# moe's last product: a stage of seven block products over pairs of token blocks, behind the first products of all nine blocks

## Chip, core and metric

One Trainium2 chip, one core. The time is the device time of one execution in microseconds, from the first to the last instruction and what lies around them; lower is better. The engines are PE (TensorE, the matrix engine), DVE (VectorE), ACT (ScalarE), POOL (GpSimd) and SP (SyncE, which issues nearly all transfers here).

## What is computed

Everything is float32: 4608 tokens, width 512.

```python
scores = scale * (q_c @ k_c.T)              # per head, in chunks of 64 tokens; 8 heads of 64
x = softmax(scores) @ v_c                   # attention, 4608 x 512
a, b = x @ w1, x @ w2                       # moe: 512 -> 1024, twice: the "first products"
y = ((a * b) @ w3) @ w_out                  # 1024 -> 1024 -> 512
h = y @ w_in                                # moe2: 512 -> 2048
out = (maximum(h, 0) + alpha * minimum(h, 0)) @ w_out2      # 2048 -> 512
```

The kernel multiplies `w3 @ w_out` once (the folds, 192 products), so that moe's last product is g = a * b (1024 wide) by one matrix of 1024 x 512.

## The kernel before

**Precision.** Every operand is held as a high and a low part in a rounded format (`split`: ScalarE copies the high part, VectorE subtracts it for the low part), and a product is three passes on PE, low x high, high x high, high x low (`PASSES`, L25). Weights come as 64-bit numbers and are converted on the chip, half a granule at a time (`convert_a` to `convert_e`, L180 to L216: one ScalarE absolute value, five VectorE operations, a ScalarE copy, two VectorE operations). There are 72 conversions: 0 to 15 for w1 and w2, 16 to 23 for w_out, 24 to 39 for w3, 32 for moe2's weights. moe2's are combined two by two (`combined_weight`, L230) into pieces for a seven-product scheme and written to DRAM.

**Tiles.** Tokens come in nine blocks of 512. A "step" (b, f) of the first products is one 128-wide slice f (of 8) of block b: `proj1` (L393) runs 12 PE products of 512 columns for a and 12 for b, ScalarE copies a out of PSUM, and `product` (L398) multiplies on VectorE. An attention unit is 256 tokens, two to a block; its scores, maximum, exponentials, normalisation, transposes and values are separate steps.

**Stages.** (1) STARTUP (L37) is an order written out by hand, one letter a step: A to E are the conversion's parts, S M X Y T P V c d attention's, a k b m a step of the first products, h s w the folds. It covers units 0 to 7, first products of blocks 0 to 3, conversions 0 to 39 and all folds; g of these blocks goes to DRAM. Sets of the first products take PSUM banks a and b and the pair p01 in turn. (2) L582 to L596: last product (`proj_wc`, L421) of blocks 0 to 3, g read back and split. (3) L598 to L627: for blocks 4 to 8, step by step, first products, attention of the next block, one conversion of moe2's weights, and the last product of the step before, straight from SBUF, into four banks (p01 and p23). y goes to DRAM. (4) moe2's first product as seven block products for eight (L654), over pairs of blocks (1,2), (3,4), (5,6), (7,8) and the two halves of block 0 (256 columns); results go to DRAM. (5) moe2's last product, seven for eight again, read from DRAM, in five output groups (L775), with the rows turned and written out (`rows`, L757).

Tiles of one tag share their buffers, and an instruction that takes a buffer waits until the last use of the one before it is over. A planner orders the instructions of each engine; PE's stand in program order where `pinned` is set, which it is from stage 2 on. Transfers of a queue issue in order.

Of the kernel before, what the change touches and what calls it, by code (L numbers as in the profile page):

```python
# [18 lines left out]
P = 128  # L19
# [25 lines left out]
    E15 a1.4 A16 B16 k1.4 b1.4 C16 D16 E16 V4 Y5 q6 m1.4 a0.6 A17 B17 k0.6 b0.6 C17 D17 E17 T5 P5 V5  # L45
    q7 m0.6 a1.5 A18 B18 k1.5 b1.5 C18 D18 E18 m1.5 a0.7 A19 B19 k0.7 b0.7 C19 D19 E19 m0.7 a1.6 A20 B20 k1.6
    b1.6 C20 D20 E20 c4 d4 c5 d5 m1.6 a1.7 A21 B21 k1.7 b1.7 C21 D21 E21 S6 M6 X6 m1.7 a2.0 A22 B22
    k2.0 b2.0 C22 D22 E22 S7 M7 Y6 X7 m2.0 a2.1 A23 B23 k2.1 b2.1 C23 D23 E23 T6 P6 V6 c6 d6 m2.1
    a2.2 A24 B24 k2.2 b2.2 C24 D24 E24 Y7 T7 P7 V7 m2.2 a2.3 A25 B25 k2.3 b2.3 C25 D25 E25 c7 d7 m2.3
    h0.0 A26 B26 C26 D26 E26 h0.1 s0 w0 A27 B27 C27 D27 E27 a2.4 A28 B28 k2.4 b2.4 C28 D28 E28 m2.4 h1.0  # L50
    A29 B29 C29 D29 E29 a2.5 A30 B30 k2.5 b2.5 C30 D30 E30 m2.5 h1.1 s1 w1 a2.6 A31 B31 k2.6 b2.6 C31 D31
    E31 m2.6 h2.0 A32 B32 C32 D32 E32 a2.7 A33 B33 k2.7 b2.7 C33 D33 E33 m2.7 h2.1 s2 w2 A34 B34 C34 D34
    E34 h3.0 A35 B35 C35 D35 E35 a3.0 A36 B36 k3.0 b3.0 C36 D36 E36 m3.0 h3.1 s3 w3 a3.1 A37 B37 k3.1 b3.1
    C37 D37 E37 m3.1 h4.0 A38 B38 C38 D38 E38 a3.2 A39 B39 k3.2 b3.2 C39 D39 E39 m3.2 h4.1 s4 w4 a3.3 k3.3
    b3.3 m3.3 h5.0 h5.1 s5 w5 a3.4 k3.4 b3.4 m3.4 h6.0 a3.5 k3.5 b3.5 m3.5 h6.1 s6 w6 a3.6 k3.6 b3.6 m3.6 h7.0 a3.7
    k3.7 b3.7 m3.7 h7.1 s7 w7
# [28 lines left out]
def tile_attention_moe_moe(ctx: ExitStack, tc: tile.TileContext, qkv: bass.AP, w12: bass.AP,  # L85
# [29 lines left out]
    g_dram = {(b, f): tc.dram_tile([P, TB], F32, name=f"g_dram{b}_{f}") for b in range(LEAD) for f in range(NF1)}  # L115
# [43 lines left out]
    def accumulators():  # L159
        p01, p23 = pair("p01", "acc"), pair("p23", "acc")  # L160
        return [p01[:, 0], p01[:, 1], p23[:, 0], p23[:, 1]]
# [8 lines left out]
    conv = [(*x, half) for x in CONVERTED if len(x) == 2 for half in range(2)] + [x for x in CONVERTED if len(x) == 3]  # L170
# [47 lines left out]
    ahead = [2 * (8 + 4 + 8)]  # L218
# [11 lines left out]
    def combined_weight(i):  # L230
# [13 lines left out]
        t14, t32 = (tmp(n).rearrange("p (g a c) -> p g a c", a=4, c=32) for n in ("t14", "t32"))  # L244
        for out, x, y in ((t14[:, left], b12, b11), (t32[:, left], b22, b12), (t32[:, right], b22, t14[:, left]),
                          (t14[:, right], b21, t32[:, right])):
            vector.tensor_tensor(out=out, in0=x, in1=y, op=ALU.subtract)
        for n, x in enumerate((t14, t32) + ((w0, b22) if half == 0 else (w1, b11))):
            g = granule((3, 5, 6, 7)[pieces[0] % 4], "wm")
            pieces[0] += 1  # L250
            if n < 3:
                split(g.rearrange("p s (g a c) -> p s g a c", a=4, c=32), x)
                nc.sync.dma_start(out=w2_dram[half, j, n], in_=g.bitcast(F32))
            else:
                split(g[:, :, :HW].rearrange("p s (g a c) -> p s g a c", a=4, c=32), x)
                nc.sync.dma_start(out=w2_dram[half, j // 2, n][:, :, HW * (j % 2):HW * (j % 2) + HW],
                                  in_=g[:, :, :HW].bitcast(F32))

    def convert():

        i = ahead[0]
        if i < len(conv):
            second_weight(i)
            if i % 2:
                combined_weight(i)
            ahead[0] = i + 1
# [11 lines left out]
    def load_unit(u, whole=True):  # L278
        if u < 4:
            slots = (24 + 2 * u, 25 + 2 * u, 2 * u, 2 * u + 1)  # L280
        elif u < 2 * LEAD:
            slots = range(24 + 4 * (u % 2), 28 + 4 * (u % 2))
        else:
            slots = (0, 1, 2, 4)
# [86 lines left out]
    wc_g = {}  # L371
    g_t, acc, ab = {}, {}, {}

    def fold(f, half):
        if half == 0:
            if f % 2 == 0:
                ab["fold"] = pair("p23", "wc")
        ps = ab["fold"][:, f % 2]
# [4 lines left out]

    def fold_split(f, lo):
        if not lo:
            wc_g[f] = granule(24 + f, "wc")
        dst, ps = wc_g[f], ab["fold"][:, f % 2]
        if lo:
            vector.tensor_tensor(out=dst[:, LO], in0=ps, in1=dst[:, HI].bitcast(F32), op=ALU.subtract)
        else:  # L390
            scalar.copy(dst[:, HI], ps)
# [6 lines left out]
    def product(b, f, a, ps):  # L398
        vector.tensor_tensor(out=a, in0=ps, in1=a, op=ALU.mult)
        if b < LEAD:  # L400
            nc.sync.dma_start(out=g_dram[b, f], in_=a)
        else:
            split_g(b, f, a)

    def empty_pair(sums, last, name, to):

        for i in (last - 1, last):
            t = tmp(name)
            (scalar.copy if i % 2 else vector.tensor_copy)(t, sums[i])
            nc.sync.dma_start(out=to(i), in_=t)  # L410
# [484 lines left out]
```

## Time and profile before

| | us |
|---|---|
| median of 3 runs | 1450.17 (1447.37 to 1450.45) |
| the profiled execution | 1448.14 |
| its span, first to last instruction | 1446.4 |
| PE busy | 1404.0 (97%) |
| VectorE busy | 1001.3 (69%) |
| ScalarE busy | 731.0 (51%) |
| mean granted clock of PE | 0.998 of full speed |

A PE product lasts longer than its distance to the next one, since they are pipelined; the distance between runs is what counts. VectorE's and ScalarE's instructions overlap a little in the same way. Idle time of an engine is given in square brackets with what ended it.

### The profile page before, as it was taken

To read this page: it belongs to the slowest core of one execution; us is meant where nothing else is said; L and a number is where in the kernel's file an instruction comes from. 1 tells how busy PE (TensorE), PEld (TensorE's weight loads), DVE (VectorE), ACT (ScalarE), POOL (GpSimd) and SP (SyncE) were. 2 spreads that over 40 slices of the span, in tenths; PEclk is the share of its full clock that TensorE was granted. 3 is DMA by queue.
4 is the path that set the end of the run, shared out by engine and by line. 5 is a ranking of instruction groups with operands and counts; after the bars stand their busy time and mean duration, and the time that the engine had idled before them with its cause. 6 is when DMAs were issued, how large, how long until landed. Compare 5 with 4: busy or idle time off the path is not lost.

```text
span 1446.4 us, 22817 instructions
## 1 busy us (share of the span) xinstructions
PE 1404.0 (97%) x8608; PEld 1163.1 (80%) x8608; DVE 1001.3 (69%) x1522; ACT 731.0 (51%) x1560; POOL 0.7 (0%) x6
## 2 busy tenths in 40 slices
PE   5899999999999999999999999999999999999997
PEld 4677788887788888888878787878898888888887
DVE  6888786233487877777245757675667878888775
ACT  6544532144355555553246767676765444444433
POOL 0000000000000000000000000000000000000000
PEclk9999999999999999999999999999999999999999
DMA  8555342344466666668372424333499563736343
GB/s 276 179 202 168 104 152 95 133 151 149 139 217 225 213 218 213 225 213 292 129 255 109 160 110 167 118 116 123 152 320 332 196 217 124 217 126 190 135 127 102
DMA packets 129790, 256.32 MB, mean 177 GB/s; under 512 B 13456, under 2 KB 58512, under 8 KB 129680
## 3 DMA queue, kind: packets, MB, share of 16 engines
q1 hardware_dynamic: 129680, 254.87, 52.1%
q8 instruction: 67, 1.10, 0.3%
q14 instruction: 43, 0.35, 0.1%
HBM read 160.44 MB, written 94.37 MB: 176 GB/s over the span
## 4 chain that ended last, share of the span: by engine, by line
PE 87%; ACT 5%; DVE 4%; DMA 3%; issue 1%; SPq 0%; ACTq 0%; DVEq 0%
PE a L128 19%; PE b L128 19%; PE q L128 17%; PE acc L128 13%; PE bc L128 9%; PE ab L128 4%; PE wc L128 3%; ACT e L77 3%; DVE m L77 1%; PE sc L128 1%; PE pa L128 1%; DVE p L77 1%; DMA g_dram<-r 1%; DMA raw<-in_w 1%; PE pa L133 1%
## 5 line engine op out<-in xcount | busy, mean ns | idle before, releaser
L128 PE MATMUL q<-op,w 128*128 128x512 f32 (+1 forms) x1020 | 219.6, 368 | 3.3 <-DVE op L77 3.3
L128 PE MATMUL acc<-gs,wc 128*128 128x512 f32 x864 | 207.7, 393 | 3.1 <-DVE gs L77 2.8
L128 PEld LDWEIGHTS q<-op,w 128*128 128x128 f32 x1020 | 178.6, 188 | 35.5 <-DVE op L77 3.7
L128 PEld LDWEIGHTS acc<-gs,wc 128*128 128x128 f32 x864 | 160.2, 188 | 40.3 <-DVE gs L77 4.9
L128 PE MATMUL a<-x,wa 128*128 128x512 f32 x672 | 166.3, 396 | 4.5 <-DVE x L77 4.5
L128 PE MATMUL b<-x,wa 128*128 128x512 f32 x672 | 163.7, 392 | 0.0
L128 PEld LDWEIGHTS a<-x,wa 128*128 128x128 f32 x672 | 127.9, 191 | 31.6 <-DVE x L77 4.8
L128 PEld LDWEIGHTS b<-x,wa 128*128 128x128 f32 x672 | 124.8, 188 | 25.9
L128 PE MATMUL bc<-yo,w 128*128 128x512 f32 (+1 forms) x600 | 133.6, 368 | 0.0
L77 ACT CAST op<-araw 128x1024 fp32r<-128x1024 f32 (+1 forms) x80 | 77.1, 966 | 96.3 <-PE q L128 32.3
L128 PEld LDWEIGHTS bc<-yo,w 128*128 128x128 f32 x600 | 105.1, 189 | 18.7
L128 PE MATMUL b<-yo,w 128*128 128x512 f32 (+1 forms) x450 | 103.9, 369 | 1.0 <-ACT t L77 1.0
L77 DVE TENSOR_TENSOR op<-araw,op 128x1024 fp32r<-128x1024 f32 (+1 forms) x80 | 88.8, 1112 | 20.7 <-ACT op L77 20.3
L128 PE MATMUL ab<-x,wa 128*128 128x512 f32 x384 | 95.1, 395 | 4.6 <-ACT a L77 4.2
L77 ACT ACTIVATE e<-sc,mx 128x64 f32<-128x64 f32 x288 | 86.3, 355 | 22.7 <-DVE mx L77 18.9
L128 PE MATMUL a<-yo,w 128*128 128x512 f32 (+1 forms) x390 | 90.6, 370 | 3.5 <-ACT p L77 2.2
L128 PEld LDWEIGHTS b<-yo,w 128*128 128x128 f32 x450 | 78.7, 189 | 16.2 <-ACT t L77 2.3
L77 ACT CAST op<-sum 128x1024 fp32r<-128x1024 f32 (+1 forms) x60 | 58.0, 966 | 62.4 <-PE q L128 45.0
L128 PEld LDWEIGHTS ab<-x,wa 128*128 128x128 f32 x384 | 70.6, 188 | 22.7 <-ACT a L77 7.9
L77 ACT COPY a<-a 128x512 f32<-128x512 f32 x56 | 33.4, 597 | 105.4 <-PE a L128 100.6
L77 DVE TENSOR_SCALAR m<-m 128x512 f32<-128x512 f32 (+1 forms) x144 | 60.5, 423 | 35.8 <-ACT m L77 35.0
L77 DVE TENSOR_TENSOR op<-sum,op 128x1024 fp32r<-128x1024 f32 (+1 forms) x60 | 66.6, 1110 | 24.9 <-ACT op L77 24.8
(121 smaller groups left out, 2104.6 us busy)
## 6 DMA issues: line engine op xcount, KB each, us to landing
araw<-g_dram SPq DMA_DIRECT2D x80, 512.0 KB, 3.8
g_dram<-r SPq DMA_DIRECT2D x144, 256.0 KB, 2.0
w_dram<-wm SPq DMA_DIRECT2D x48, 512.0 KB, 3.4
w<-w_dram SPq DMA_DIRECT2D x48, 512.0 KB, 5.3
qk<-in_qkv SPq DMA_DIRECT2D x36, 512.0 KB, 5.6
raw<-in_w2nd SPq DMA_DIRECT2D x32, 512.0 KB, 4.1
y_dram<-y SPq DMA_DIRECT2D x36, 256.0 KB, 3.3
raw<-in_w SPq DMA_DIRECT2D x16, 512.0 KB, 4.3
```

The costliest lines, as they stand in the source:

```text
L77: ins = f(*args, **kw)
L128: ins = nc.tensor.matmul(*args, **kw)
L133: ins = nc.tensor.transpose(*args, **kw)
```

## The change

- moe's last product becomes a stage of its own, behind the first products of all nine blocks. It takes token blocks in pairs and multiplies quarters: 7 block products of 24 PE products each in place of 8. Five groups: the halves of block 0 first (256 columns), then the four pairs. g goes to DRAM from every step and is read back as in stage 5; sums and differences are formed on VectorE and split there. y goes to DRAM.
- STARTUP ends behind block 1. Blocks 2 to 8 run in one loop, with units 6 to 17 placed at set half steps and w3's conversions, the folds and moe2's conversions spread over blocks 2 to 8: ten conversions in each of blocks 2 and 3, then 7, 7, 6, 6, 2. A fold is issued two conversions behind its own.
- The folded matrix is combined into pieces like moe2's and goes through DRAM; its 14 tiles are loaded during block 8.
- The PSUM pair p01 becomes two single banks, c and d.
- moe2's first operands and weights are loaded during the last groups of the new stage; later weights one or two passes ahead.
- The output rows of the last wide pair are issued half from SP and half from POOL.

```diff
-LEAD = 4
-CONVERTED = [(w, i) for w, n in (("a", 8), ("o", 4), ("c", 8)) for i in range(n)]
-CONVERTED += [("m", j + i, half) for half in range(2) for j in range(8) for i in (0, 8)]
+FIRST = [(w, i, half) for w, n in (("a", 8), ("o", 4)) for i in range(n) for half in range(2)]
+FOLDED = [("c", i, half) for i in (0, 4, 1, 5, 2, 6, 3, 7) for half in range(2)]
+SECOND = [("m", j + i, half) for half in range(2) for j in range(8) for i in (0, 8)]
+CONVERTED = FIRST + FOLDED[:4] + SECOND[:2] + FOLDED[4:12] + SECOND[2:4] + FOLDED[12:] + SECOND[4:]
...
+        while folds and folds[0] <= i - 2:
+            fold(folds.pop(0))
...
+    def fold(i):
+        f, half = conv[i][1:]
+        j = f % 4
+        if half == 0 and f < 4:
+            ab["fold"] = pair("p23", "wc")
+        ps = ab["fold"][:, f // 4]
...
+        if half and f >= 4:
+            w0, w1 = tmp("wf"), ps
+            scalar.copy(w0, ab["fold"][:, 0])
...
+            sums_of_quads(t14, t32, w0[:, left], w0[:, right], w1[:, left], w1[:, right], left, right)
+            pieces_out((t14, t32, w1, w0[:, left]), lambda g: g, lambda n: wc_dram[n, j if n < 3 else j // 2], j % 2)
...
     def product(b, f, a, ps):
         vector.tensor_tensor(out=a, in0=ps, in1=a, op=ALU.mult)
-        if b < LEAD:
-            nc.sync.dma_start(out=g_dram[b, f], in_=a)
-        else:
-            split_g(b, f, a)
+        h, m = divmod(f, 4)
+        nc.sync.dma_start(out=g_dram[b, h, m // 2][:, m % 2], in_=a)
...
-            if sets % 2:
-                pp = pair("p01", "ab")
-                ab[tuple(rest)] = [pp[:, 0], pp[:, 1], None]
-            else:
-                ab[tuple(rest)] = [bank("a"), bank("b"), None]
+            ab[tuple(rest)] = [bank(n) for n in ("cd" if sets % 2 else "ab")] + [None]
...
+    CONVERSIONS = {4: 7, 5: 7, 6: 6, 7: 6, 8: 2}
     pinned[0] = True
...
+    for b in range(2, NB):
+        parts = {}
+        if b + 1 < NB:
+            for i, places in enumerate(((0, 1, 4, 6), (8, 9, 12, 13)) if b < 4 else ((0, 1, 6, 8), (4, 5, 10, 12))):
+                parts.update(unit_parts(2 * (b + 1) + i, places))
         for f in range(NF1):
...
+            pa, pb = (bank(n) for n in ("cd" if sets % 2 else "ab"))
+            sets += 1
             proj1(b, f, 0, pa)
             a = tmp("a")
             scalar.copy(a, pa)
+            parts.get(2 * f, lambda: None)()
             proj1(b, f, 1, pb)
             product(b, f, a, pb)
+            parts.get(2 * f + 1, lambda: None)()
+            n = CONVERSIONS.get(b, 0)
+            for _ in range(1 + (f in (3, 4)) if b < 4 else n * (f + 1) // NF1 - n * f // NF1 if b < NB - 1 else f < n):
                 convert()
+            if (b, f) == (3, NF1 - 1):
+                while folds:
+                    fold(folds.pop(0))
+                load_unit(11)
+            if b == NB - 1:
+                for at in LOADS[f]:
+                    moe_weights(*at)
...
+    EARLY = {2: (-1,), 3: ORDER[:4], 4: ORDER[4:]}
...
+    for n, s in enumerate(groups):
...
+        for m in range(NM):
+            a21, a22 = raw(s, 2, m), raw(s, 3, m)
+            sm = slot(cycle("sum", SUMS), "sum", F32)[:, :, :w]
+            add(sm, a21, a22)
+            sums.append(sm)
+            o4 = spread(a22)
+            o5 = spread(sm)
...
+            multiply(o4, m, 1, p4, m == 0, m == NM - 1)
+            multiply(o5, m, 0, p5, m == 0, False)
...
+        if n == len(PAIRS):
+            weights(0, 0)
+        for m in range(NM):
+            a11, a21 = raw(s, 0, m), raw(s, 2, m)
+            add(a21, a11, a21, ALU.subtract)
+            o1 = spread(a11)
+            o7 = spread(a21)
...
+            multiply(o1, m, 4, p1, m == 0, False)
+            multiply(o7, m, 2, p7, m == 0, m == NM - 1)
+            add(sums[m], sums[m], a11, ALU.subtract)
+            o6 = spread(sums[m])
...
+            multiply(o6, m, 3, p6, m == 0, m == NM - 1)
...
+        for m in range(NM):
+            a12 = raw(s, 1, m)
+            multiply(spread(a12), m, 5, p1, False, m == NM - 1)
+            add(sums[m], a12, sums[m], ALU.subtract)
+            multiply(spread(sums[m]), m, 6, p5, False, m == NM - 1)
...
+        closing = [close]
+        for o in EARLY.get(n, ()):
+            load_y(0) if o < 0 else operand(o)
...
-        if j == 2 and s + 1 < len(wide):
+        if j == (2 if s else 4) and s + 1 < len(wide):
             load_y(s + 1)
+        if turn in (0, 1):
+            for k in range(2):
+                weights(0, 2 * turn + 4 + k)
...
-            bc = pair(("att", "p01", "p23")[(2 * turn + i) % 3], "bc")
-            b[i], c[i] = (bc[:, h] for h in range(2))
+            which = (2 * turn + i) % 3
+            bc = pair("att" if which == 0 else "p23", "bc") if which != 1 else None
+            b[i], c[i] = (bc[:, h] for h in range(2)) if bc is not None else (bank(n) for n in "cd")
...
-            nc.sync.dma_start(out=out[r:r + P, a * P:(a + 1) * P].rearrange("(b r) c -> r b c", r=32),
+            queue = nc.gpsimd if s == len(PAIRS) - 1 and a % 2 else nc.sync
+            queue.dma_start(out=out[r:r + P, a * P:(a + 1) * P].rearrange("(b r) c -> r b c", r=32),
```

Here `spread` splits a 1024-wide operand (ScalarE high part, VectorE low part), `raw` reads 1024 columns of g from DRAM with three reads ahead, `multiply` runs 12 PE products, and `pieces_out` splits a combination's pieces and writes them to DRAM. NM is 2 in the new stage and 4 in moe2's.

## Rows read from the trace of the kernel before

**Rows 1.** Page, first part: busy time, share of the span, instructions.
```profile
PE 1404.0 (97%) x8608; PEld 1163.1 (80%) x8608; DVE 1001.3 (69%) x1522; ACT 731.0 (51%) x1560; POOL 0.7 (0%) x6
```
**Rows 2.** Chain that ended last: start us, us, what.
```profile
408.51 2.72 PE a L128 x12
...
444.69 2.72 PE a L128 x12
...
1062.19 2.88 PE bc L128 x24
...
1186.22 8.16 PE q L128 x36
...
1262.38 8.16 PE q L128 x36
```
**Rows 3.** Tile wa, PE, to 150 us: ns min/median/max, first and last start.
```profile
L128 PE MATMUL ab<-x,wa x192: 387/389/501, 38.2 to 142.7; 128*128 128x512 f32 x192
```
**Rows 4.** PE's timeline: start us, us, engine, line, operation, out<-in, count, idle before.
```profile
284.51 3.03 PE L128 MATMUL acc<-gs,wc 128*128 128x512 f32 x12
...
380.24 2.88 PE L128 MATMUL a<-x,wa 128*128 128x512 f32 x12
...
419.32 1.16 PE L128 MATMUL sc<-qk 64*64 64x64 f32 x64
...
738.85 1.52 PE L128 MATMUL a<-yo,w 128*128 128x512 f32 x6
...
1413.89 1.70 PE L128 MATMUL q<-op,w 128*128 128x256 f32 x12 [2.25 <-DVE op L77]
1416.60 1.70 PE L128 MATMUL q<-op,w 128*128 128x256 f32 x12 [1.01 <-DVE op L77]
...
1439.73 2.04 PE L133 MATMUL tr<-ident,post 128*128 128x128 f32 x16
```
**Rows 5.** Stretches: us; PE, PEld, DVE, ACT, POOL busy; clock, DMA share, GB/s.
```profile
142.75:200.00 57.25, 55.23 (x462) 44.09 (x461) 48.05 (x88) 28.48 (x96) 0.00 (x0) 1.00 0.37 123
...
380.24:738.85 358.61, 357.76 (x2542) 294.22 (x2540) 257.28 (x473) 166.77 (x466) 0.00 (x0) 1.00 0.63 214
408.51:444.69 36.18, 36.18 (x282) 29.76 (x281) 29.04 (x56) 18.23 (x54) 0.00 (x0) 1.00 0.64 219
...
1050.00:1100.00 50.00, 50.00 (x380) 48.30 (x380) 35.09 (x59) 32.37 (x54) 0.00 (x0) 1.00 0.94 322
1186.22:1262.38 76.16, 76.16 (x337) 63.06 (x337) 63.42 (x68) 32.90 (x33) 0.00 (x0) 1.00 0.52 165
```
**Rows 6.** Groups by form: busy us, mean ns of one; idle before, releasers.
```profile
L128 PE MATMUL acc<-gs,wc 128*128 128x512 f32 x864 | 207.7, 393 | 3.1 <-DVE gs L77 2.8 <-ACT y L77 0.2
```
**Rows 7.** VectorE's timeline: one conversion, one combination's first parts, a normalisation.
```profile
187.84 0.42 DVE L77 TENSOR_SCALAR m<-m 128x512 f32<-128x512 f32 x1
...
191.03 0.68 DVE L77 TENSOR_TENSOR m<-m,w 128x512 f32<-128x512 f32 x1
191.64 0.42 DVE L77 TENSOR_SCALAR m<-m 128x512 f32<-128x512 f32 x1
...
414.60 0.75 DVE L77 TENSOR_TENSOR t<-m 128x256 f32<-128x256 f32 x2
415.27 0.42 DVE L77 TENSOR_TENSOR t<-m,t 128x256 f32<-128x256 f32 x1
...
428.69 1.22 DVE L77 TENSOR_TENSOR e<-e,sm 128x1024 f32<-128x1024 f32 x1
429.83 0.68 DVE L77 TENSOR_TENSOR gs<-a,gs 128x512 fp32r<-128x512 f32 x1
```
**Rows 8.** Waits, 142.75 to 284.5: us in total, times, longest.
```profile
PEld ab L128 <- ACT a L77: 3.5, 8, 1.2
```
**Rows 9.** SP's issues: start us, us, line, what, count.
```profile
1403.12 6.18 SPq L767 DMA_DIRECT2D out<-o  x8
...
1409.40 14.36 SPq L725 DMA_DIRECT2D araw<-g_dram  x10
```

More of the change, by code (lines that the diff above doesn't have):

```diff
@@ L368, in attn_out @@
             scalar.copy(xs[HI], pa)
[L371 to L378, printed above, removed]
+    ab = {}
+    def fold(i):
[4 more added lines that the diff above has]
+        ps = ab["fold"][:, f // 4]
         for k in range(4):
@@ L510, in tile_attention_moe_moe @@
     head[0] = True
[L511 removed]
+    lent = {1: "p23", 3: "p23", 5: "p23"}
     sets = 0
@@ new lines, in tile_attention_moe_moe, with copied, cycle, raw @@
+            if b == NB - 1:
+                for at in LOADS[f]:
+                    moe_weights(*at)
+    EARLY = {2: (-1,), 3: ORDER[:4], 4: ORDER[4:]}
+    turns = Counter()
+    def copied(out, x):
+        ins = scalar.copy(out, x)
+        if ordered[0]:
+            tc.keep_in_program_order(ins)
+    ordered = [False]
+    def cycle(kind, places):
+        turns[kind] += 1
+        return places[(turns[kind] - 1) % len(places)]
+    def raw(s, q, m):
+        while reads and len(fetched) < 3:
+            fetched.append((reads.pop(0), slot(cycle("raw", RAWS), "araw", F32)))
+            at, t = fetched[-1]
+            fetch(t[:, :, :wide[at[0]]], *at)
+        at, t = fetched.pop(0)
+        return t[:, :, :wide[s]]
@@ new lines, in spread, with multiply @@
+    def spread(x):
+        h, l = (slot(p, "op")[:, :, :x.shape[2]] for p in cycle("op", OPS))
+        copied(h, x)
+        add(l, x, h.bitcast(F32), ALU.subtract)
+        return h, l
+    def multiply(x, m, o, ps, first, last):
+        w = moe_weight if NM < 4 else weight
+        for k in range(2):
+            for e in range(2):
+                for i, (a, h) in enumerate(PASSES):
+                    matmul(ps[e] if isinstance(ps, list) else ps[:, e], w[2 * m + k, o][a][:, e * P:(e + 1) * P], x[h][:, k],
+                           start=first and m + k + i == 0, stop=m == NM - 1 and k == 1 and i == 2,
+                           skip_group_check=not (first and last))
@@ L629, in tile_attention_moe_moe, with products @@
+    close()
+    ordered[0] = False
+    for j in range(2, NJ // 2):
         weights(0, j)
-    def product(s, j, o, ps, first, last):
+    def products(s, j, o, ps, first, last):
         for k in range(2):
@@ L662, in both @@
             for n, k in enumerate(jj[i]):
-                product(s, k, o, ps[:, n * w:(n + 1) * w], first and n == 0, last)
+                products(s, k, o, ps[:, n * w:(n + 1) * w], first and n == 0, last)
         def keep(name, i):
@@ L719, in tile_attention_moe_moe, with fetch @@
     fetched = []
-    def raw(s, q, m):
-        while reads and len(fetched) < 3:
-            fetched.append((reads.pop(0), slot(turn("raw", RAWS), "araw", F32)))
-            at, t = fetched[-1]
-            nc.sync.dma_start(out=t[:, :, :wide[at[0]]], in_=g2_dram[at])
-        at, t = fetched.pop(0)
-        return t[:, :, :wide[s]]
-    def spread(x):
-        h, l = (slot(p, "op")[:, :, :x.shape[2]] for p in turn("op", OPS))
-        copied(h, x)
-        add(l, x, h.bitcast(F32), ALU.subtract)
-        return h, l
-    def multiply(x, m, o, ps, first, last):
-        for k in range(2):
-            for e in range(2):
-                for i, (a, h) in enumerate(PASSES):
-                    matmul(ps[e] if isinstance(ps, list) else ps[:, e], weight[2 * m + k, o][a][:, e * P:(e + 1) * P], x[h][:, k],
-                           start=first and m + k + i == 0, stop=m == 3 and k == 1 and i == 2,
-                           skip_group_check=not (first and last))
+    def fetch(t, s, q, m):
+        nc.sync.dma_start(out=t, in_=g2_dram[s, q, m])
     def turned(s, c, half, tag, t):
@@ L799, in tile_attention_moe_moe @@
             done = done[2:]
-        p7, p1 = (pair(q, "q")[:, :, :w] for q in (qc, "p01"))
+        p7, p1 = pair(qc, "q")[:, :, :w], [bank(q)[:, :w] for q in "cd"]
         for m in range(NM):
```

259 lines of the change are left out of this document (128 added, 131 removed).

## The prediction

> **What bounds the kernel now.** Read the page's busy times first: the matrix engine (PE) 97%, VectorE 69%, ScalarE 51% [rows 1]. Busy alone says little, so next the chain that ended last: from 408.51 to 444.69 it is an unbroken sequence of twelve-product runs of 2.72 us; a 256-column run of 24 takes 2.88; one output group takes 76.16 [rows 2]. So a 512-column product costs 2.72/12 = 0.2267 us, a 256-column one 0.12. Four steps of three runs are 32.64 us of that 36.18, so one attention unit costs PE 3.54. The output group is 336 products, 336 x 0.2267 = 76.17: no loss at all.
>
> Third, the stages. Blocks 0 and 1 are finished at 142.8 (eight of their sixteen sets lie in the pair, 192 products, the last of which starts at 142.7 [rows 3]); the last product by itself starts at 284.51, the loop over blocks 4 to 8 at 380.24, moe2 at 738.85, the last group ends at 1439.73 [rows 4]. Against the price list: 142.8 to 284.5 holds 576 products (130.6) and two units less a little (6.8), so 4.3 of 141.7 are lost, 3.1%. 284.5 to 380.2 holds 372 (84.3) and two units (7.1): 4.3 lost of 95.7. 380.2 to 738.9 holds 1452 (329.1) and eight units (28.3): 1.2 lost of 358.6, 0.3%, with VectorE busy 257.28 of it, or 29.04 of 36.18, 80% [rows 5]. PE sets the time nearly everywhere; what the others could do is break it.
>
> **The products.** Today's 864 last products [rows 6] are 864 x 0.2267 = 195.9 us. After: four groups of seven block products of 24, 672 x 0.2267 = 152.3, and block 0's group of 168 at 256 columns, 20.2. Saved: 23.4. First products, folds and attention keep their counts. Between 142.8 and moe2 PE's work then is 56 steps of 24 and 192 fold products, 1536 x 0.2267 = 348.2, twelve units 42.5, and 172.5: 563.2, where now 596.1 pass. **Term 1: -32.9**, of which 23.4 are work and the rest today's losses; the new losses are added below.
>
> **Blocks 2 to 8.** VectorE's instructions follow each other in less than they last: a conversion's seven take 187.84 to 191.64 = 3.80 us, one of 512 columns 0.61, two of 256 columns 0.67, one of 1024 1.14 [rows 7]. A w3 conversion is 3.8, one for moe2 (one instruction less) 3.2, one combination of a pair 4 x 0.335 + 3 x 0.61 + 0.34 = 3.5, a unit 4.0. Blocks 2 and 3 each hold 8 x 3.8 + 2 x 3.2 + 3 x 3.5 + 8 x 0.61 + 2 x 4.0 = 60.2 of PE's 43.5 + 7.1 + 21.8 (folds) = 72.4: 83%. Blocks 4 and 5: 7 x 3.2 + 3.5 x 3.5 + 4.9 + 8.0 = 47.6 of 50.6: 94%. Blocks 6 and 7: 42.6 of 50.6, 84%. Block 8: some 15 of 43.5. The DMA load of block 4: seven raw loads of 0.52 MB, 3.5 x 1.83 MB of pieces, eight g writes of 0.26, two units of 1.57: 15.3 MB in 50.6, or 303 GB/s, where the loop has 219 at a DMA share of 0.64 and a later stretch 322 at 0.94 without PE idling [rows 5]. So nothing is over its limit, but two things come near theirs together, and what now hides a late conversion is thinner.
>
> The lower bound of the loss is today's loop, 0.3% (1). The upper one is the stretch behind 142.8 where VectorE is busy 48.05 of 57.25, 84% [rows 5]: 208 products and most of two units are 53.7, so 3.6 lost, 6.7%, which over 390.7 is 26. Part of that should not come back: eight waits of PE's weight loads on ScalarE's copy of a (3.5 us [rows 8]) belong to the pair's second bank, which waits for the reading of the first; single banks a, b, c, d do not share a tile. I take the 3.1% of 142.8 to 284.5 for blocks 2 to 5 (246 us) and 0.3% for the rest. **Term 2: +8** (1 to 26). In it: unit 6's transposes stand four runs and its scores behind the start of its scores, 12.0 us, and the chain of a unit today runs from 419.32 [rows 4] to 429.91, the end of the normalisation [rows 7], 10.6; fold (1, 0) of a new pair waits for the pieces of the last one, read out of the same two banks; the last two folds of block 3 wait for conversions issued just ahead.
>
> **The start.** Two conversions (22, 23) move ahead of block 1's last step, 7.6 us of VectorE, which is nearly full there; unit 6's scores go behind it. If VectorE sets that end, 7.6; if PE does and the pair's waits go, -1. **Term 3: +4**, in the middle.
>
> **The new stage.** Per group VectorE has 27 operations of 1024 and two of 512: 27 x 1.14 + 1.2 = 32.0 of 38.1, 84%; the output group is the same work doubled and has VectorE at 63.42 of 76.16 with no loss [rows 5]. The group after pair (3, 4) gets load_y's three additions (92%), that of (7, 8) four operands (96%). The lower bound is 0; the upper one five group changes at the 2.25 of the one late operand in today's last group [rows 4], 11. **Term 4: +4**: one such wait where the narrow group goes over to a wide one, and some 1 in each of the two full groups. The raw reads are the ones the output group makes, at 165 GB/s; moe's weights (14 loads, 7.3 MB) lie in block 8, with VectorE and DMA at ease. moe2's first two weights come during the last group's final 10.9 us, later ones 19 us a pass ahead of use: 0; if they were late, one wait of 5.
>
> **The last group.** On SP eight output writes take up to 6.18 us to issue, and the raw reads come behind them at 1409.40 [rows 9]; PE then waits 2.25 and 1.01 [rows 4], and the group takes 44.2 (1395.5 to 1439.7) for 336 x 0.12 = 40.3. Half of the writes go to POOL's queue, about 8 us of SP's. **Term 5: -3** (-3.9 to +3: no row shows what a write costs on POOL). Here the Trainium skill speaks against the change: "DMA: Bandwidth & Descriptors", section "Issuing engines are not separate DMA queues", says that a second issuing engine saves only the sequencer's time, which is usually small beside the transfer. Taken at its word this term would be 0 and the forecast 1431; the row has the reads late by the issue itself, so I stay with it.
>
> moe2's first stage keeps its products, its 7 us of losses at the changes of operands and its order; its third pair becomes two banks: 0.
>
> **Sum:** -32.9 + 8 + 4 + 4 - 3 = -19.9. The profiled execution took 1448.14 (span 1446.4), so 1428.2; it lies 2 below the median of 1450.17, within the spread of the three runs. I predict **1428**.
>
> **Rivals.**
> *Clean.* The loop runs as today's at 80%, the stage as the output stage: terms 2 and 4 near 1 and 0, term 3 near 0: -32.9 + 1 + 0 - 3 = -35, so 1413, with small losses up to 1420. For it: two stretches without loss at 80% and 83%. Against: 94% in blocks 4 and 5.
> *VectorE and DMA set blocks 2 to 7.* The loss is 6.7% throughout, 26: 1446; with half of it above the forecast, 1435 to 1447. For it: the one stretch at 84% that lost that. Against: most of that loss was the shared pair.
> *Slower: folds in PE's fixed order.* Each of the sixteen folds stands in PE's order two conversions behind its own; when VectorE is late, PE stands there, with all first products behind it, and so all copies and g writes. Without term 2 the sum is -27.9, so it decides where the folds alone cost over 31, that is from 2 us a fold on: 1451 and more. Against: a conversion's chain is some 7 us and two steps give 12; block 2 is at 83%.
> *POOL's writes are held up.* The output tiles then stay occupied, VectorE's row turns wait, and the last group loses again what it loses now: +3.9 in place of -3: 1435. The Trainium skill, "SBUF — State Buffer", section "Who interferes with whom", has VectorE instructions with two SBUF inputs contend with GpSimd's reads, and nearly all in that group are such; no row shows POOL at work there.
> *No effect.* The 23.4 are not saved only if PE were not what ends last; the rows above exclude it, short of the saturation case, whose upper end is no change.
>
> **Chances.** Forecast (1420 to 1436) 0.54, POOL's hold-up in it 0.08; clean (below 1420) 0.17; saturation (1436 to 1447) 0.16; within 0.2% of 1450.17, about what a measurement here tells from no change (1447.3 to 1453.1), 0.05; slower 0.08, nearly all by the folds. So faster 0.87. The range 1412 to 1444 leaves out some 0.05 below and 0.15 above; the likeliest case alone is 1420 to 1436.
>
> **What the new profile would show.** Term 1: 672 and 168 products in place of 864, each wide group at 38.1. Term 2: from the first step of block 2 to the last of block 8 about 399, and the waits named above beside folds and the first unit. Term 3: block 2's first product near 147. Term 4: five groups in 176 to 177. Term 5: the last group near 41, writes issued from POOL. Wrong would be: VectorE over 95% in blocks 4 to 7 with PE's gaps spread over all steps; PE standing at each fold; or a gap of several us ahead of moe2.

## The result and the profile after

The changed kernel takes 1429.74 us (median of 4 runs, 1427.54 to 1431.08) against 1448.77 (1447.03 to 1450.45) for the kernel before on the same chip: a ratio of 0.987, 95% interval 0.986 to 0.989. It is faster by 19 us. The forecast was 1428, with 1412 to 1444.

The profiled execution took 1429.92 us, its span 1428.1. The page's first part, beside [rows 1]:

```profile
PE 1379.2 (97%) x8584; PEld 1149.2 (80%) x8584; DVE 1088.6 (76%) x1601; ACT 767.4 (54%) x1597; POOL 9.5 (1%) x22
```

PE lost 24.8 us of busy time and 24 instructions, VectorE gained 87, ScalarE 36. POOL now has work. PE's groups by form between 545 and 721 us answer to [rows 6]:

```profile
L124 PE MATMUL q<-op,w 128*128 128x512 f32 x288 | 69.2, 389 | 0.0
L124 PE MATMUL a<-op,w 128*128 128x512 f32 x96 | 27.1, 391 | 1.4 <-DVE op L70 1.4
...
L124 PE MATMUL q<-op,w 128*128 128x256 f32 x72 | 9.6, 283 | 0.0
L124 PE MATMUL b<-op,w 128*128 128x256 f32 x24 | 4.2, 283 | 0.0
```

With a, b, c and d alike these are 288 + 4 x 96 = 672 products of 512 columns and 72 + 4 x 24 = 168 of 256, in place of 864. PE's timeline at the starts of the stages and at the waits that PE has from block 2 on, up to moe2's first turns (the first line is block 2's first product; the number in brackets is PE's idle time):

```profile
139.03 1.29 PE L124 MATMUL a<-x,wa 128*128 128x512 f32 x5
...
156.03 1.06 PE L129 MATMUL pa<-ident,e 128*128 128x128 f32 x8 [1.92 <-DVE e L70]
...
200.53 1.65 PE L124 MATMUL wc<-wo,w 128*128 128x512 f32 x6 [2.72 <-DVE w L70]
...
275.39 1.88 PE L124 MATMUL wc<-wo,w 128*128 128x512 f32 x7 [2.24 <-DVE w L70]
...
372.45 1.16 PE L124 MATMUL pa<-pt,v 64*64 64x64 f32 x64 [2.15 <-ACT pt L70]
373.54 4.63 PE L124 MATMUL b<-x,wa 128*128 128x512 f32 x12
...
427.38 1.31 PE L124 MATMUL pa<-pt,v 64*64 64x64 f32 x64 [2.65 <-ACT pt L70]
428.63 4.39 PE L124 MATMUL b<-x,wa 128*128 128x512 f32 x12
...
545.50 0.52 PE L124 MATMUL a<-op,w 128*128 128x256 f32 x3
...
631.86 0.50 PE L124 MATMUL c<-op,w 128*128 128x512 f32 x1 [0.74 <-DVE op L70]
...
660.73 0.50 PE L124 MATMUL a<-op,w 128*128 128x512 f32 x1 [1.36 <-DVE op L70]
...
720.74 1.52 PE L124 MATMUL a<-yo,w 128*128 128x512 f32 x6
...
759.95 1.66 PE L124 MATMUL a<-yo,w 128*128 128x512 f32 x6 [0.49 <-ACT t L70]
...
765.71 1.66 PE L124 MATMUL a<-yo,w 128*128 128x512 f32 x6 [1.15 <-ACT p L70]
...
1075.62 0.86 PE L124 MATMUL a<-op,w 128*128 128x512 f32 x3
...
1421.17 2.10 PE L129 MATMUL tr<-ident,post 128*128 128x128 f32 x16
```

From these starts, and the prediction's own prices:

| stretch of PE | forecast | measured |
|---|---|---|
| up to block 2's first product (142.8 before) | 146.8 | 139.0 |
| blocks 2 to 8: work 390.7, and the loss | + 8 | + 15.8 (406.5) |
| new stage: work 172.5, and the loss | + 4 | + 2.7 (175.2) |
| moe2's first stage (738.85 to 1090.83 before, 352.0) | 352.0 | 354.9 |
| last stage (to 1439.73 before, 348.9) | 345.9 | 345.6 |

The tail behind 1421.17 is 6.9 us, where 6.7 stood behind 1439.73. Against before that is -3.8 + (406.5 + 175.2 - 596.1 = -14.4) + 2.9 - 3.3 + 0.3 = -18.3, the difference of the spans, 1446.4 and 1428.1. The row of the start is the least certain: in the traces of the eleven other kernels below whose start has the same code, block 2 begins between 136.9 and 142.4, so that -3.8 is known to some 3 us and no better.

The same stretches as windows of after, with the columns of [rows 5]; the second line is block 4:

```profile
139.03:545.50 406.47, 394.78 (x3170) 323.01 (x3168) 314.49 (x616) 197.34 (x620) 0.00 (x0) 0.99 0.74 257
291.53:342.12 50.59, 50.59 (x465) 41.48 (x464) 41.84 (x84) 29.34 (x98) 0.00 (x0) 1.00 0.92 316
...
545.50:720.74 175.24, 173.13 (x842) 146.14 (x840) 152.21 (x147) 88.21 (x107) 0.00 (x0) 1.00 0.68 235
720.74:1075.62 354.88, 348.97 (x1681) 291.50 (x1680) 227.62 (x313) 251.86 (x424) 0.00 (x0) 1.00 0.48 173
```

Block 4 has no loss at all, with DMA at a share of 0.92 and VectorE at 41.84 of 50.59, 83%; the prediction had counted 94%. By PE's waits and starts the loss lies in block 2 (5.1), block 3 (2.6), block 5 (3.8) and block 6 (4.2); 7 and 8 lose nothing.

Half of the last group's writes now come from POOL. SP's and POOL's timelines at the same pair of row tiles, beside [rows 9]:

```profile
1383.45 1.80 SPq L839 DMA_DIRECT2D out<-o  x4
...
1385.96 2.03 SPq L839 DMA_DIRECT2D out<-o  x4
```
```profile
1383.72 2.17 POOL L839 DMA_DIRECT2D out<-o  x4 [6.26 <-DVE o L70]
1386.18 2.17 POOL L839 DMA_DIRECT2D out<-o  x4 [0.29 <-DVE o L70]
```

SP spends some 0.5 us on each of its four, POOL 0.54, side by side. PE has no wait in that group, where it had 2.25 and 1.01 in [rows 4].

### The profile page after: what moved, and what is told of

Its sections match the earlier page's. It is cut to its first block, busy times and chain, and to the rows that moved or that the text cites. A ratio compares the mean times of both kernels' runs of the same rounds, so it can differ in the third digit from the quotient of the medians.

```text
span 1428.1 us, 23134 instructions
## 1 busy us (share of the span) xinstructions
PE 1379.2 (97%) x8584; PEld 1149.2 (80%) x8584; DVE 1088.6 (76%) x1601; ACT 767.4 (54%) x1597; POOL 9.5 (1%) x22
## 4 chain that ended last, share of the span: by engine, by line
PE 72%; DVE 12%; DMA 6%; ACT 6%; issue 3%; SPq 1%; ACTq 0%; DVEq 0%
PE b L124 15%; PE a L124 14%; PE q L124 14%; PE d L124 10%; PE c L124 9%; PE bc L124 6%; ACT e L70 4%; DVE m L70 3%; PE wc L124 3%; DVE p L70 2%; DMA raw<-in_w 1%; DMA yq<-y_dram 1%; DVE wm L70 1%; PE pa L124 1%; DMA araw<-g_dram 1%
## 5 line engine op out<-in xcount | busy, mean ns | idle before, releaser
L124 PE MATMUL b<-x,wa 128*128 128x512 f32 x432 | 110.0, 405 | 0.0
L124 PE MATMUL a<-x,wa 128*128 128x512 f32 x432 | 104.5, 390 | 3.5 <-DVE x L70 3.5
L124 PE MATMUL d<-x,wa 128*128 128x512 f32 x432 | 105.2, 392 | 0.4 <-DVE wa L70 0.4
L124 PE MATMUL c<-x,wa 128*128 128x512 f32 x432 | 104.5, 390 | 0.0
L124 PEld LDWEIGHTS a<-yo,w 128*128 128x128 f32 x438 | 76.9, 188 | 22.2 <-ACT p L70 5.0
L124 PEld LDWEIGHTS c<-x,wa 128*128 128x128 f32 x432 | 80.9, 188 | 16.9
L124 PEld LDWEIGHTS d<-x,wa 128*128 128x128 f32 x432 | 80.2, 188 | 16.8 <-DVE wa L70 0.5
L124 PE MATMUL c<-op,w 128*128 128x512 f32 (+1 forms) x345 | 89.7, 368 | 0.7 <-DVE op L70 0.7
L124 PE MATMUL d<-op,w 128*128 128x512 f32 (+1 forms) x345 | 89.6, 368 | 0.0
L124 PE MATMUL a<-op,w 128*128 128x512 f32 (+1 forms) x315 | 81.9, 368 | 1.4 <-DVE op L70 1.4
```

The lines of the kernel that those rows point to most:

```text
L124: ins = nc.tensor.matmul(*args, **kw)
```

## The experiments

Twelve kernels, each the changed kernel or the even spread of the second experiment, with one or a few edits. Ratios are to the kernel before; the stretches and waits are those of one trace a kernel.

**1. Blocks 5 and 6: the order on ScalarE.** At the wait of block 5, the timelines of ScalarE, VectorE and SP:

```profile
362.61 0.66 ACT L70 ACTIVATE m<-raw 128x512 f32<-128x512 f32 x1 [0.99 <-DMA raw<-in_w2nd]
...
366.15 0.31 ACT L70 ACTIVATE e<-sc,mx 128x64 f32<-128x64 f32 x1 [2.37 <-DVE mx L70]
...
371.27 1.13 ACT L70 COPY pt<-pa 128x1024 f32<-128x1024 f32 x1
```
```profile
355.61 0.18 DVE L70 TENSOR_SCALAR sm<-sm 128x16 f32<-128x16 f32 x1 [4.38 <-ACT e L70]
...
358.00 0.68 DVE L70 SCALAR_TENSOR_TENSOR p<-raw,p 128x512 f32<-128x512 uint32 x1
...
363.81 0.69 DVE L70 TENSOR_TENSOR wm<-t,wm 128x512 fp32r<-128x512 f32 x1 [0.98 <-ACT wm L70]
364.42 1.22 DVE L70 TENSOR_REDUCE mx<-sc 128x16 f32<-128x1024 f32 x1
```
```profile
358.71 0.33 SPq L171 DMA_DIRECT2D raw<-in_w2nd  x1
```

ScalarE waits 0.99 for a raw load; its split of a piece is late; VectorE waits for that split, and the maximum stands behind it; the exponentials wait 2.37 for the maximum, and the other unit's copy pt, for which PE stands, comes behind all of them. The load itself is late by VectorE: SP issues it at 358.71, once VectorE has read a raw buffer (358.00), and VectorE had stood 4.38 us, to 355.61, for the first unit's exponentials. So: is it the order (two units interleaved) or the load?

```diff
-... else ((0, 1, 6, 8), (4, 5, 10, 12))
+... else ((0, 1, 5, 6), (7, 8, 12, 13))
```

> Only the half steps of the two units in blocks 4 to 7 are changed, so that the first unit's transposes and values (5, 6) come ahead of the second unit's scores (7). Theory (ScalarE's order: the copy of the turned exponentials stands behind the other unit's sixteen exponentials): the two waits of 2.15 and 2.65 us in blocks 5 and 6 go, and with them the two slow runs behind them (1.6 each), so blocks 5 and 6 take 50.6 each in place of 54.4 and 54.8 and the time falls by 8, to 1422. Rival (VectorE and DMA are too full in these blocks): the loss only moves to other waits in blocks 4 to 7, and the time stays within 3 of 1429.7.

1432.16 us (1429.36 to 1434.54), 0.988 [0.986, 0.990]. Waits stand at 366.33 (1.09), 386.68 (1.32), 398.01 (0.72) and 422.05 (2.49, on pt again). The loss only changed its place: this other order does not take it away. My theory fell.

**2. Fewer conversions in blocks 4 to 7.**

```diff
-    CONVERSIONS = {4: 7, 5: 7, 6: 6, 7: 6, 8: 2}
+    CONVERSIONS = {4: 6, 5: 6, 6: 5, 7: 5, 8: 6}
```

> Only the number of moe2 conversions in blocks 4 to 8 is changed, from 7, 7, 6, 6, 2 to 6, 6, 5, 5, 6; VectorE's load in blocks 4 and 5 falls from 94% to 84% and in 6 and 7 from 84% to 74%. Rival of the first run (saturation): blocks 5 and 6 lose nothing any more, 1422, unless block 8 at 80% loses. Theory (ScalarE's order): the order of the two units is as it was, so the waits for the copy stay, 1427 to 1431.

1423.59 us (1422.67 to 1424.94), 0.983 [0.981, 0.984], and no wait of PE between 279.1 and the new stage: blocks 4 to 8 lose nothing. The waits of blocks 2 and 3 (1.92, 2.46, 2.22) stay. Fewer conversions in blocks 4 to 7 take the waits away. It is not a block's own count that decides: block 6 of the changed kernel broke with six, and blocks 4 and 5 of the even spread hold six without a wait (more behind experiment 9).

**3. The shared pair back.** Here `cd()` gives the two halves of `pair("p01")`, in the startup and the last stages too.

```diff
-            pa, pb = (bank(n) for n in ("cd" if sets % 2 else "ab"))
+            pa, pb = cd() if sets % 2 else [bank(n) for n in "ab"]
```

> Banks c and d are again the two halves of one tile, everywhere; all else is the changed kernel. Theory (a second product run into a pair waits for ScalarE's reading of the first half): in 28 of the 56 steps of blocks 2 to 8, where PE's order is fixed, and in 8 of the start, PE waits some 0.9 us: the loop grows by some 25 and the start goes back from 139 to about 143, so 1455 to 1462, slower than the kernel before. Rival (the start came earlier for another reason, and the waits of before were VectorE's): within 4 of 1429.7.

1489.07 us (1482.33 to 1489.85), 1.027 [1.024, 1.029], slower than before. Its waits from 148 to 607 us (engine, tile and line; who released it; us in total, times, longest):

```profile
PEld cd L124 <- ACT a L70: 56.5, 22, 9.4
PE cd L124 <- ACT a L70: 47.9, 22, 9.0
```

Block 2 starts at 148.69, the loop takes 458.3. So without the single banks this order of work would lose the whole gain three times over: about 10 us at the start and 52 in the loop. It is far more than the kernel before lost with the same pair. There PE's order has other products between two runs into the pair (a run into ab at 188.07, four fold products at 190.79, the next run into ab at 191.76); the new loop issues b right behind a, while ScalarE still has to read a out of the same tile (that this is the reason for the size is argued from the order, not tried).

**4. All output rows from SP.**

```diff
-            queue = nc.gpsimd if s == len(PAIRS) - 1 and a % 2 else nc.sync
+            queue = nc.sync
```

> All output rows are issued from SP again; all else is the changed kernel. Theory (SP's issue time held up the raw reads): the last group takes 44 in place of 41 again, 1433. Rival (the transfers, not their issue, set it): the last group as it is, 1430.

1434.08 us (1431.06 to 1436.83), 0.989 [0.987, 0.991]. The last stage takes 351.2 in place of 345.6, and PE stands in the last group again; SP's timeline, then PE's:

```profile
1390.94 3.70 SPq L839 DMA_DIRECT2D out<-o  x8
1394.74 10.76 SPq L812 DMA_DIRECT2D araw<-g_dram  x7
```
```profile
1403.80 2.45 PE L124 MATMUL q<-op,w 128*128 128x256 f32 x12 [2.75 <-DVE op L70]
```

The write issues ahead of the raw reads are the cause, as term 5 had it; the half on POOL is worth 4.3 us in the median, 5.6 in the stage. The Trainium skill, "DMA: Bandwidth & Descriptors", section "Issuing engines are not separate DMA queues", gives a second engine the sequencer's time alone and calls it usually small. The trace agrees on what is saved, and disagrees on the size here, where reads stand behind eight issues.

**5. Block 2's folds.**

```diff
-            for _ in range(1 + (f in (3, 4)) if b < 4 ...
+            for _ in range(1 + (f in ((0, 7) if b == 2 else (3, 4))) if b < 4 ...
```

> In block 2 alone the two steps that take a second conversion are the first and the last (0 and 7) in place of 3 and 4; block 3 stays. Theory (each of the two fold waits is VectorE's pile of two combinations and a doubled conversion behind one step): the wait of 2.7 us in block 2 goes, the one of 2.2 in block 3 stays; 1427. Rival (a fold stands too close behind its own conversion wherever it is): both stay, or block 2's moves to another fold; 1430.

1435.26 us (1432.18 to 1440.54), 0.991 [0.989, 0.994]: new waits of 3.30 and 1.98 at 152.59 and 155.8, 0.86 left of the one at 200.5, and larger waits in blocks 5 and 6 (the longest 3.96). With the doubled steps at these places the very first fold meets a late conversion; experiment 12 has places at which block 2's folds do not wait.

**6. moe2's first stage: the place of y's load.**

```diff
-        if j == (2 if s else 4) and s + 1 < len(wide):
+        if j == 2 and s + 1 < len(wide):
```

> Only the place of load_y in moe2's first pair of blocks goes back from j = 4 to j = 2. moe2's first stage took 354.9 in place of 352.0, with new waits at 759.95 and 765.71. Theory (load_y's three additions and reads fall among the leaky parts of that turn): the stage takes 352 to 353 again, 1427 to 1428. Rival (its weights, which now come one or two passes ahead on SP's queue, hold up the result writes): unchanged, 354 to 355.

1429.54 us (1427.97 to 1439.76), 0.988 [0.984, 0.991]; the stage takes 354.6, a wait of 1.23 stands at 746.71 in place of the two at 760. No gain, as the rival had it; experiment 11 tries the rival's reason.

**7 and 8. What of the load breaks blocks 5 and 6?** The even spread, with every g tile of blocks 4 to 7 written a second time (7), or one more VectorE operation of 512 columns in each step (8).

```diff
+        if 4 <= b < 8:      # 7
+            nc.sync.dma_start(out=tc.dram_tile([P, TB], F32, name=f"spare{b}_{f}"), in_=a)
+        if 4 <= b < 8:      # 8
+            vector.tensor_tensor(out=a, in0=a, in1=a, op=ALU.max)
```

> The kernel with 6, 6, 5, 5, 6 conversions (1423.6), and in blocks 4 to 7 each g tile is also written to a spare tile in DRAM: 2.1 MB a block more, so that the DMA load (316 and 288 GB/s by tile sizes) stands above that of the changed kernel (303 and 275), with VectorE as light as in that run. If DMA is what broke blocks 5 and 6, 4 to 8 of loss come back: 1428 to 1432. If VectorE is, 1423 to 1425.

> The same kernel with 6, 6, 5, 5, 6 conversions, and in blocks 4 to 7 each step has one more VectorE operation of 512 columns (the maximum of the product with itself, in place), which brings VectorE back to 94% and 84%, with the DMA load as light as in that run. If VectorE is what broke blocks 5 and 6, 4 to 8 come back: 1428 to 1432. If DMA is, 1423 to 1425.

1420.49 us (1418.09 to 1426.1), 0.981 [0.978, 0.983], and 1422.31 (1416.55 to 1431.05), 0.982 [0.978, 0.986]. Neither has a wait in blocks 4 to 8, and neither is slower than the even spread in the median (8's traced loop is, 404.3 to 399.5, but in blocks 2 and 3 alone). Neither load alone does it. Experiment 7 does more than the even spread and came out 3 us under it, with intervals that overlap: differences of 3 us between these kernels are not shown by the times alone.

**9. Both loads.**

> As the even spread (6, 6, 5, 5, 6 conversions), with both added loads at once in blocks 4 to 7: every step's g tile is written to DRAM a second time, to a spare tile that nothing reads, and every step has one more in-place VectorE operation of 512 columns on that tile (a maximum with itself, 0.61 us). By the rows that makes VectorE 44.1 + 4.9 = 49.0 of 50.6 us in blocks 4 and 5 (97%, the changed kernel has 94%) and DMA about 15.9 MB in 50.6 us, 314 GB/s (the changed kernel 303). Theory, the two loads together are what breaks blocks 5 and 6 of the changed kernel: blocks 5 and 6 lose some 8 us again, with waits on ScalarE's copy pt, and the time is 1430 or more. Rival, the number of conversions does it (the chain of raw load, seven tmp tiles, ScalarE's splits and piece writes has 50.6 us for seven and cannot hold it), however busy VectorE and DMA are: no waits from block 4 on, and the time is that of the even spread with either load alone, 1419 to 1425.

1427.91 us (1422.4 to 1431.4), 0.986 [0.983, 0.988], between theory and rival. (The expectation's 44.1 us for six conversions should be 42.6 by the prediction's prices.) One break of the known kind, in block 7, on PE's timeline:

```profile
474.95 1.20 PE L124 MATMUL pa<-pt,v 64*64 64x64 f32 x64 [2.53 <-ACT pt L70]
476.07 4.53 PE L124 MATMUL b<-x,wa 128*128 128x512 f32 x12
```

and 0.23 in block 5; a window from 2.3 us behind its start has DMA above that of the changed kernel's block 4, and VectorE at 44.83 of 51.00, 88%:

```profile
345.00:396.00 51.00, 50.77 (x466) 41.61 (x465) 44.83 (x87) 27.36 (x94) 0.00 (x0) 1.00 0.95 331
```

So a break came back with both loads, in one trace, and with neither alone. But the load of a block does not tell which block breaks: blocks 4 and 5 of this run hold with VectorE busy 44.6 and 44.7 us and DMA shares of 0.93 and 0.95, and block 7 breaks at 0.85. What does tell is how late the normalisation of the block's first unit starts on VectorE, counted from the block's first product on PE (in the changed kernel 302.41, 355.61, 410.62 and 462.02, behind 291.53, 342.12, 396.56 and 451.39):

| us | block 4 | block 5 | block 6 | block 7 |
|---|---|---|---|---|
| changed kernel | 10.9 | 13.5, breaks | 14.1, breaks | 10.6 |
| even spread | 10.8 | 10.7 | 11.2 | 10.4 |
| experiment 8 | 10.9 | 11.5 | 12.8 | 11.5 |
| experiment 9 | 10.9 | 11.9 | 12.5 | 14.8, breaks |

In the eleven traces with this order of the units (all but those of experiments 1 and 3) it starts at 13.5 us or later in nine blocks, and all nine break; in the other 35 it starts at 12.8 or earlier, and none of them loses more than 0.3. Blocks 5 and 6 of the changed kernel are the two that follow a block of seven conversions. So the break looks like work carried over from the block before. This is read from the traces; no run was made for it, and how the added loads and the conversions' own chain (raw load, ScalarE's splits, seven tmp tiles, the writes of pieces) share in the delay stays open.

**10 and 12. Room for the waits of blocks 2 and 3**, on the even spread. In 10 the first unit is transposed a half step later and block 3's doubled steps are 2, 3 and 4, with none at 7; in 12 the unit again, and block 2's doubled steps are 2 and 3.

```diff
-            for i, places in enumerate(((0, 1, 4, 6), (8, 9, 12, 13)) if b < 4 ...
+            for i, places in enumerate(((0, 1, 5, 6), (8, 9, 12, 13)) if b < 4 ...
-            for _ in range(1 + (f in (3, 4)) if b < 4 ...
+            for _ in range(1 + (f in (3, 4)) if b < 3 else 1 + (f in (2, 3, 4)) - (f == 7) if b < 4 ...     # 10
+            for _ in range(1 + (f in ((2, 3) if b == 2 else (3, 4))) if b < 4 ...                           # 12
```

> As the even spread, and two waits of blocks 2 and 3 given room: the first unit of blocks 2 and 3 is transposed one half step later, and block 3's doubled steps are 2, 3 and 4 with no conversion at its last step, so that its last folds stand one whole step behind their conversion. Theory, these two waits (1.9 us at unit 6's transposes, 2.2 at the last folds) are each a distance that is a little too short: both go, no other appears, and the time is 1423.6 - 4 = 1419.5. Rival, blocks 2 and 3 (VectorE 83% busy by the prediction's count) are behind by that much at any place, as two earlier shifts of places showed: waits of 1.5 to 3 us appear at other folds or transposes, and the time is 1422 to 1426.

> As the even spread, with unit 6's and unit 8's transposes one half step later, block 3's doubled steps as in the change (3 and 4), and block 2's doubled steps at 2 and 3 in place of 3 and 4. In the even spread's rows the first half of a new pair of w3 granules is converted straight behind a moe2 combination and a unit's normalisation, and its low part is ready at 204.12, where PE stands for it from 201.8 to 204.26 (2.46 us); with the doubling one step earlier that conversion has a step of its own behind the combination's. Theory, the two waits of block 2 (1.9 and 2.5 us) are local queues on VectorE of this length: both go, the wait of 2.2 at block 3's last folds stays, and the time is 1423.6 - 4.4 = 1419. Rival, blocks 2 and 3 as a whole run behind, and a wait taken out at one step comes up again at the next fold, as for the three shifts of places before: 1421 to 1425, with a new wait of 2 us or more at another fold of block 2.

10: 1421.75 us (1421.0 to 1423.27), 0.982 [0.981, 0.983]. The unit's wait is gone; block 2's 2.46 stays, and the 2.2 of block 3's fold became 3.52 and 1.24. Its loop is no shorter than the even spread's (402.1 to 399.5); what it gains in the trace lies in the start, whose code is the same (138.4 to 141.4), and in moe2's first stage (351.5 to 354.6, below). 12: 1420.34 us (1417.91 to 1423.8), 0.981 [0.979, 0.983]. Both waits of block 2 are gone, and the next unit stands:

```profile
192.72 1.94 PE L129 MATMUL pa<-ident,e 128*128 128x128 f32 x8 [2.92 <-DVE e L70]
```

In both a new wait came for the old ones, as the rivals had it; the times lie between the forecasts of theory and rival. The shifts of 10 and 12 pay 1.8 and 3.3 us in the median, those of 1 and 5 cost 2.4 and 5.5. 12 is the best version with the reference's work alone, but its interval overlaps the even spread's: that it beats that one is not shown.

**11. moe2's first weights from POOL**, on the even spread.

```diff
-        weights(0, j)
+        weights(0, j, queue=nc.gpsimd)
...
-                weights(0, 2 * turn + 4 + k)
+                weights(0, 2 * turn + 4 + k, queue=nc.gpsimd)
```

> As the even spread, and the weights of moe2 that are loaded just ahead of its first stage and in its first two turns (w2_dram, twelve sets 2 to 7 of four or three tiles) are issued from POOL in place of SP. Theory, they stand on SP's queue ahead of the writes of the stage's first results, so that the tiles of those results come free late; that is the two waits of 0.5 and 1.2 us on ScalarE's tiles t and p in the changed kernel: both go, the stage takes 352 to 353 as in the kernel before in place of 354.6, and the time is some 2 us under the even spread, 1421 to 1422. Rival, the loads' own transfers hold the writes up, whoever issues them, or the waits come from ScalarE's order: the stage still takes 354 to 355 and the time is 1423 to 1425.

1429.02 us (1426.49 to 1431.54), 0.987 [0.986, 0.989], slower than the even spread by 5 us. The waits near 760 are gone, but a wait of 8.00 stands at 727.45, and the stage takes 361.5. VectorE's timeline and a window of it name the reason:

```profile
724.43 1.23 DVE L70 TENSOR_TENSOR ysum<-yq 128x1024 f32<-128x1024 f32 x1 [10.75 <-DMA yq<-y_dram]
```
```profile
712.00:724.40 12.40, 7.45 (x33) 5.82 (x31) 1.68 (x2) 1.55 (x3) 1.15 (x3) 0.97 1.00 372
```

Eleven loads of 0.5 MB went out from POOL between 699 and 713, each as soon as its tile was free; the DMA engines are full (share 1.00), and the three loads of the next y took a median of 13.4 us to land where they take 6.5 in the changed kernel. In this run those loads of y also went out earlier, at 707 to 714 in place of 748 to 750, and their sum stands in VectorE's order 13.3 us behind the stage's start, where the changed kernel has it 35.2 behind; VectorE stood 10.75 us for them, ScalarE behind VectorE, and PE behind ScalarE. Theory and rival both missed that. How much of the 8.00 is the full engines and how much the new place of the sum is not separated. But it shows where to look: VectorE's sum of y in the changed kernel, and then in experiment 10:

```profile
755.92 1.23 DVE L70 TENSOR_TENSOR ysum<-yq 128x1024 f32<-128x1024 f32 x1 [2.52 <-DMA yq<-y_dram]
```
```profile
747.83 1.22 DVE L70 TENSOR_TENSOR ysum<-yq 128x1024 f32<-128x1024 f32 x1 [0.24 <-DMA yq<-y_dram]
```

In 10, whose moe2 stage is the same code, y is there 2.3 us earlier, neither wait near 760 exists, and the stage takes 351.5 us. With 1.00 at this place (experiment 7) it takes 353.0, with 1.60 (12) 354.2, with 1.95 (the even spread) 354.6, with 2.52 (the changed kernel) 354.9; experiments 1, 4, 5, 8 and 9 lie between (1.07 to 2.47, 353.6 to 354.7). Only experiment 6, with 0.42 and 354.6, is out of line: there the sums stand elsewhere in VectorE's order. That the late y is what costs these 3 us is read from this row of traces; no edit of its own tried it.

## Why the prediction came out right, and where its terms were off

**The work saved (term 1)** is as computed: 672 and 168 products, and a new stage of 175.2 us. These 23.4 us are the gain. Of the rest, the kernel before lost 9.5 us in the same stretches, and the new kernel loses 18.5 there (15.8 and 2.7).

**Blocks 2 to 8 (term 2, +8)** cost 15.8, inside its bounds of 1 and 26; the forecast was half of it. Of the waits that the prediction named, the one at unit 6's transposes is there as named (1.92). The fold of a new pair, (1, 0), waits 2.72, but for the low part of its own weights (w), not for the pieces of the last pair. The last folds of block 3 do not wait at all: the 2.24 at 275.39 stands at fold (3, 0), again the first of a new pair, in the same step of its block. In both places the conversion for which PE stands comes on VectorE behind two combinations (in block 2 from 186.73 to 197.98, the low part at 199.79), and in experiment 12 the wait of block 2 is gone with its doubled steps one step earlier. The three waits are 6.9 us together. What the prediction missed is blocks 5 and 6, 8.0 us. It named blocks 4 and 5 as the place where VectorE and DMA come near their limits together, but put a flat 3.1% on them; block 4 lost nothing, and 5 and 6 lost two breaks, where a delay runs through ScalarE's and VectorE's orders into one unit's copy. With the even spread the loss is 399.5 - 390.7 = 8.8.

VectorE's count there was wrong as well: 94% forecast, 83% measured in block 4. The 3.80 us for a conversion, from the stretch in [rows 7], hold short waits between its instructions; here the second starts 0.73 behind the first, where such an instruction elsewhere takes 0.61:

```profile
189.23 0.69 DVE L77 SCALAR_TENSOR_TENSOR m<-raw,m 128x512 uint32<-128x512 uint32 x1
189.96 0.43 DVE L77 TENSOR_SCALAR p<-m 128x512 uint32<-128x512 uint32 x1
```

Without them a conversion for moe2 is 3 x 0.33 + 3 x 0.61 = 2.8 in place of 3.2, and the count 88%. The rest is work that had not been done: block 4 has 84 of the 90 VectorE instructions that its steps hold, and block 5 has 91 (44.95 us). Blocks 2 and 3 have 6 and 10 folds, not 8 each as the prediction took it, since a fold comes two conversions behind its own; VectorE is busy 84% and 75% of them, where 83% was counted for each. The prediction looked for the trouble in two engines that come near their limits together. Busy shares do not tell where the stretch breaks (experiments 8 and 9); the delay that the first unit of a block finds does.

**The start (term 3, +4)** has the wrong sign: -3.8. The two conversions may well have cost what was said: with the pair back, block 2 starts at 148.7, 5.9 us later than before, near the upper bound of 7.6. But the single banks give back 9.7 there (one trace each; with the spread of the starts, 6 to 12); the prediction had granted the pair's waits 1 us at this place and none in the sum. The measured -3.8 lies outside the two bounds that it gave, 7.6 and -1. This error and term 2's cancel: together they were forecast at +12 and came out at +12.0. That the total came so near is luck to this extent: two terms off by 8 us each, in opposite directions.

**The new stage (term 4, +4)** cost 2.7, with one short wait in each of the two groups that the prediction called full: 0.74 and 1.36 us, against its 1 each.

**moe2's first stage (0)** cost 2.9. The prediction looked at its weights and its products and not at the load of the next y, whose sum stands in VectorE's order ahead of results that PE waits for (read from the traces, experiment 11).

**The last group (term 5, -3)**: -3.3 over the stage, and experiment 4 shows the mechanism. The rule of the Trainium skill that is quoted there, taken at its word, would have left these 3 us in place. POOL's writes were not held up: 0.54 us an issue beside VectorE's work on two SBUF inputs, as against 0.53 for its loads in experiment 11. The contention that the Trainium skill, "SBUF — State Buffer", section "Who interferes with whom", describes was not to be seen here in PE's time. Whether the issue of a write reads SBUF in the sense of that section, no run here shows.

Of the rivals, the clean case failed by blocks 2, 3, 5 and 6; saturation in its strict form, a loss of 6.7% throughout, failed by block 4 (no loss at a DMA share of 0.92) and experiments 7 and 8; the folds cost 2.2 to 2.7 where they stand, over the 2 us from which they would have decided, but only two of sixteen do.

## What to carry over

A loop that issues two runs of products back to back needs each in a tile of its own: here that was worth some 60 us, more than the change itself. When an in-order loop breaks at single places, look for the delay in the stretch ahead of the break, and take work out of that stretch (the even spread, 6 us, no wait left) before shifting places, which moved the waits in experiments 1, 5 and 10 and in part of 12. Before a load moves to another queue, ask what it will overtake, and what will move up on the queue that it leaves.

## What was unexpected on the chip

The granted clock fell after two of the waits and not after others of the same length. Windows of after, behind the break of block 5, that of block 6, and the wait at 156:

```profile
372.40:378.00 5.60, 5.55 (x76) 4.56 (x77) 5.60 (x14) 2.76 (x6) 0.00 (x0) 0.70 0.88 301
427.30:432.90 5.60, 5.52 (x77) 4.58 (x78) 5.16 (x10) 2.42 (x5) 0.00 (x0) 0.70 0.76 274
156.00:160.00 4.00, 3.97 (x22) 3.44 (x23) 4.00 (x9) 2.27 (x4) 0.00 (x0) 1.00 0.25 91
```

A mean of 0.70 lies between the levels 1.2 and 2.4 GHz. In the first two PE came out of waits of 2.15 and 2.65 us into 64 products of 64 x 64, and the next run of twelve took 4.46 and 4.23 us to the run behind it, where 2.72 is usual; so each break cost 1.5 to 1.7 us beyond its wait. Behind the 1.92 us at 156 (transposes, then full products) and the folds' 2.24 and 2.72 the runs kept their length. Experiment 12's 2.92 was followed by transposes of 1.94 us in place of 1.06. So it looks as if small products behind a wait made the difference, but other runs speak against that: at the same fold of block 2, with full products behind the wait, experiments 6 and 8 (in this order) have

```profile
200.76 4.14 PE L124 MATMUL wc<-wo,w 128*128 128x512 f32 x10 [2.46 <-DVE w L70]
...
205.57 4.64 PE L124 MATMUL wc<-wo,w 128*128 128x512 f32 x10 [2.78 <-DVE w L70]
```

where ten such products take 2.56 in the changed kernel. The mean granted clock behind these two waits was 0.64 over 4.8 us and 0.50, the lower level throughout, over 5.5 us. So behind waits of 2 to 3 us the clock fell in one execution and not in another with the same code; what decides it these runs do not show. The same wait can therefore cost 1.5 to 2 us more in one trace than in the next.
